# A linear and a sliding-window attention stack with its gradients on one core: another schedule for the window attention's backward, and phi's derivative made from stored features

## The chip, the core and the metric

The kernel runs on 1 of the 8 cores of one Trainium2 chip, in one launch. The metric is the device time of one execution in microseconds (us), of which several are taken; the median counts. A core has five engines that run their own instruction queues in order and wait for each other by semaphores: TensorE (matmuls, PE in the profile), VectorE (DVE), ScalarE (ACT), GpSimd (POOL) and SyncE (SP, which here only issues DMAs). ScalarE's queue issues some of the DMAs too. TensorE writes into PSUM, which has eight banks of 2 KB in each partition; VectorE and ScalarE read it from there.

## The reference

Four residual layers on x of shape [2048, 640], in the order A, B, A, B, with the weights of A used twice and those of B twice; then the gradients of x and of the four weight matrices by reverse differentiation, from a given `grad_out`. 32 heads of 20 columns each.

```python
def _A_ref(x, wqkv, wo):                       # linear attention
    q, k, v = ...                              # [32 heads, 2048, 20] each, of x @ wqkv
    phi = lambda t: jnp.where(t > 0, t + 1, jnp.exp(t)) + 1e-6
    pq, pk = phi(q), phi(k)
    kv = jnp.einsum("bhsd,bhse->bhde", pk, v)
    z = jnp.einsum("bhsd->bhd", pk)
    num = jnp.einsum("bhqd,bhde->bhqe", pq, kv)
    den = jnp.einsum("bhqd,bhd->bhq", pq, z)[..., None] + 1e-6
    return (num / den) ... @ wo

def _B_ref(x, wqkv, wo):                       # softmax attention, causal window of 256
    scores = jnp.einsum("bhqd,bhkd->bhqk", q, k) * (Dh ** -0.5)
    mask = (idx[:, None] - idx[None, :] >= 0) & (idx[:, None] - idx[None, :] < W)
    p = _softmax(jnp.where(mask[None, None], scores, -1e9), axis=-1)
    return jnp.einsum("bhqk,bhkd->bhqd", p, v) ... @ wo

x = x + _A_ref(_layernorm(x), A_wqkv, A_wo)    # and B, A, B in the same way
```

The derivative of phi is 1 where t > 0 and exp(t) elsewhere, that is min(exp(t), 1).

## The kernel before, in words

The 2048 rows are 16 tiles of 128 rows (index `tt`). Everything is bf16 with sums in float32. Layers count 0 (A), 1 (B), 2 (A), 3 (B).

**Forward (`forward`).** All work is recorded as operations with an engine, a guessed duration and what they read and write; `Sched` then plans them against each other and writes out the order of every engine (`emit`). Guessed times and the order in which operations were recorded decide, so taking some out can move others. For an A layer `a_qkv` makes the projections of a tile in chunks of 320 columns: ScalarE takes exp (L462), VectorE caps it at 1 (L463), which gives `e` = phi's derivative, and adds max(t, 1e-6) (L466), which gives the features. Features of q (`pq`), features of k beside v (`kv`), and `e` itself (320 KB a tile, L475) are stored to DRAM from SP's queue for the backward.

**Backward.** It alternates between a `bwd_phase` and the attention's backward `B_attn_bwd`: phase for layer 3, attention of layer 3, phase (layer 3's tail, layer 2, the start of layer 1), attention of layer 1, phase (layer 1's tail and layer 0). `bwd_phase` is planned by `Sched` as well. In it `lin_grads` makes dq, dk and dv of an A layer for each tile: six chunks of banded matmuls (L856), of which VectorE multiplies those of q and k by `e` (L1190) and ScalarE copies those of v (L1186). Before them `start` brings `dNT`, `kvT` and `ee` (the stored `e`, 320 KB) in by SP's queue. `tail` follows: `dh` by TensorE and ScalarE (L849, L997), then `scr` and `sm` on VectorE (L1005 to L1011), `w` on ScalarE (L1012), `gw` on GpSimd (L1015) and the carried gradient `gcar` on VectorE (L1017). In layer 2 `local_dO` comes behind it for the attention of layer 1: `slab` and `dd` on VectorE (L1058 to L1072), `prod` on GpSimd (L1065), and a store of `dOp` from ScalarE's queue (L1075).

**The attention's backward (`B_attn_bwd`).** Its order is written out by hand. Heads go in 8 groups of four. Within a group the steps are 15 blocks `n`, each of three 128x128 pieces of the band for four heads; a block has two pairs of heads, `h = 2n + p`. For each pair:

- `mm_s` makes scores into the tile `pair{h % 3}` (two banks, three such tiles), `act_exp` takes exp on ScalarE (L1351), GpSimd masks two of the three pieces (L1355, L1358).
- `mm_dp` writes dP over the scores, and `dve_ds` on VectorE (L1366) makes `ds` = exp x dP x scale in bf16.
- `ds` has to be transposed for dq: by `pe_turn` on TensorE (six transposes, L1384) into `dsT_ps` (two buffers of one bank), copied to SBUF by `copy_t` on VectorE or ScalarE (L1387), or by `dma_turn`, a DMA transpose on SP's queue. `by_dma` says for which blocks the second pair goes by DMA.
- The products (L1399, L1403) are narrow sums of 32 columns for dq, dk and dv. `pair_acc` lays them in the spare columns 384 to 480 of the tile `pair` that two pairs later holds scores and dP, and `pair_evac` takes them out to `dqkv` (128x120, L1387), on ScalarE or VectorE.

Each of these is given a place in time by a number of pairs in `ORDER`; they are sorted by it, and that is the order in every engine's queue. The loop that issues them:

Of the kernel before, what the change touches and what calls it, by code (L numbers as in the profile page):

```python
# [32 lines left out]
def dve_ns(n):  # L33
# [4 lines left out]
    ((0.3, 1.05, "ACT", 0.6, 1.6, "DVE"), (1.3, 2.25, "DVE", 0.6, 1.6, "ACT"), (2.3, 3.5, "DVE", 0.6, 1.05, "ACT")),  # L38
    ((0.7, 2.25, "DVE", 0.6, 1.3, "ACT"), (0.3, 1.8, "ACT", 0.6, 1.3, "ACT"), (2.05, 1.8, "DVE", 0.25, 1.3, "ACT")),
# [140 lines left out]
class Kern:  # L180
    def __init__(self, ctx, tc, x0, A_wqkv, A_wo, B_wqkv, B_wo, grad_out, outs):
# [69 lines left out]
        for l in (0, 2):  # L251
            self.sv[l] = dict(
                pq=d.tile([T, D], BF, name=f"pq{l}"), e=d.tile([T, 2 * D], BF, name=f"e{l}"),
# [57 lines left out]
    def forward(self):  # L311
# [7 lines left out]
        with ExitStack() as st:  # L319
# [120 lines left out]
            def a_qkv(l, tt, hnT):  # L440
# [3 lines left out]
                def chunk(ci):  # L444
                    def f():
# [362 lines left out]
    def bwd_phase(self, lb, la, nb, ahead=()):  # L808
# [8 lines left out]
        with ExitStack() as st:  # L817
# [82 lines left out]
            if wide:  # L900
                for name, n, shape, dt in (
                        ("dh", 1, [P, D], F32), ("w", 1, [P, D], F32), ("gw", 1, [P, D], F32), ("sm", 3, [P, 8], F32),
                        ("scr", 1, [P, D], BF), ("pq", 2, [P, D], BF), ("dNT", 2, [P, DT + 1, P], BF),
                        ("kvT", 2, [P, 2 * DT, P], BF), ("ee", 2, [P, 2 * D], BF)):
# [248 lines left out]
            def lin_grads(tt, items, t0):  # L1153
# [3 lines left out]

                def start():
# [4 lines left out]
                    c["ee"] = load("ee", sv["e"], tt)  # L1163

                def chunk(kind, ci):
                    def f():
# [18 lines left out]
                        if kind == "v":  # L1185
                            op("ACT", act_ns(CW), lambda: nc.scalar.copy(dst(), ps.t[:, 0:CW]), [ps],  # L1186
                               [("dqkv", tt, "v")])
                        else:
                            e, x0 = c["ee"], (D if kind == "k" else 0) + e0
                            op("DVE", dve_ns(CW), lambda: nc.vector.tensor_mul(dst(), ps.t[:, 0:CW], e.t[:, x0:x0 + CW]),  # L1190
                               [ps, e], [("dqkv", tt, kind)])
# [99 lines left out]
    def B_attn_bwd(self, l, dqkv, slab0=None, first=None):  # L1291
        nc, tc, D, T, TT, H, G, DP = self.nc, self.tc, self.D, self.T, self.TT, self.H, self.G, self.DP
        ld, E, DS, PR, TPS, TSB, ACC = {}, {}, {}, {}, {}, {}, {}
        with ExitStack() as st:
# [75 lines left out]
            def by_dma(n):  # L1370
                return n % NB not in (0, 2, 4, 6) and n < NS - 6
# [34 lines left out]
            def spare(h):  # L1406

                return PR[h][:, :, 3 * P:3 * P + 3 * HPAD].rearrange("p i (s c) -> p i s c", c=HPAD)

            def pair_acc(g, t, p, h):  # L1410
                if h not in PR:
                    PR[h] = pps.tile([P, 2, 512], F32, name=f"pair{h % 3}")
# [143 lines left out]
```

## Time and profile before

| | |
|---|---|
| median of 3 runs | 2328.52 us (2324.72 to 2328.61) |
| the profiled execution | 2327.18 us, of which the span from first to last instruction is 2325.2 us |
| mean granted TensorE clock | 0.945 |
| busy: PE, weight load | 2023.2 us (87%), 1405.2 us (60%) |
| busy: DVE, ACT, POOL | 1463.7 us (63%), 1182.6 us (51%), 852.3 us (37%) |
| DMA | 389.22 MB, 167 GB/s on the mean |
| attention backward, layers 3 and 1 | from 849.5 and from 1619 us, some 320 us each |
| `lin_grads` of layers 2 and 0 | from about 1381 and 2150 us |

Rows of groups read: line of the kernel, engine, operation, out<-in with shapes, count | busy us, mean ns of one | idle time of the engine just before them, and what ended it. A row of a timeline is start in us, duration in us, engine, line, operation, and in brackets how long the engine had been idle and for whom. A row of stretches gives, after start, end and length, busy us and count of PE, weight load, DVE, ACT and POOL, then granted clock, the busy share of the DMA engines and GB/s; asked for one line alone, it has that engine alone. Rows of waits give the waiting engine, tile and line, what it waited for, us in total, times and the longest. In a row of one line's instructions stand minimum, median and maximum in ns. A busy PE is not PE at its peak, since the ends of pipelined matmuls are modelled.

### The profile page before, as it was taken

What the parts mean: (1) busy time and instruction counts of PE and PEld (TensorE: products, weight loads), DVE (VectorE), ACT (ScalarE), POOL (GpSimd) and SP (SyncE); (2) the same over time, 40 slices, a digit from 0 to 9 for tenths busy, and PEclk for the clock granted to TensorE, in tenths of its full rate; (3) what the DMA queues carried; (4) which work ended last, traced back from release to release, by engine and by line L of the source; (5) the groups of instructions that cost most, each with busy time, mean ns of one, the idle gap of its engine ahead of it and who ended that gap; (6) DMA issues with size and microseconds to landing.
All of it is one profiled execution on the core that took longest, in us unless ns stands there. A gap on an engine that the chain in (4) does not pass through costs nothing. (4 is left out here: it accounts for less than half of the span.)

```text
span 2325.2 us, 67576 instructions
## 1 busy us (share of the span) xinstructions
PE 2023.2 (87%) x27798; PEld 1405.2 (60%) x27798; DVE 1463.7 (63%) x3048; ACT 1182.6 (51%) x2091; POOL 852.3 (37%) x1851
## 2 busy tenths in 40 slices
PE   6879899888887688888889979997888888998999
PEld 4556566555555456666656657754666665665674
DVE  6657677555564488898943328912998885443551
ACT  4527787527787137787832213311888783210330
POOL 1015455315666245555522203311555552221120
PEclk9989999879999798899999989998999899998999
DMA  7658999646675768898887789737898988987973
GB/s 256 198 140 192 209 203 216 169 125 161 151 157 126 197 165 150 136 155 147 155 192 171 160 191 196 181 85 157 147 151 148 148 147 171 193 187 177 214 171 100
DMA packets 968103, 389.22 MB, mean 167 GB/s; under 512 B 860401, under 2 KB 939889, under 8 KB 967537
## 3 DMA queue, kind: packets, MB, share of 16 engines
q1 hardware_dynamic: 931488, 351.24, 72.7%
q10 hardware_dynamic: 36304, 33.67, 4.5%
q8 instruction: 217, 3.56, 0.7%
q14 instruction: 94, 0.76, 0.1%
HBM read 115.34 MB, written 114.95 MB: 99 GB/s over the span
## 5 line engine op out<-in xcount | busy, mean ns | idle before, releaser
L1366 DVE SCALAR_TENSOR_TENSOR ds_sb<-pair,e_sb 128x768 bf16<-128x768 f32 x480 | 457.5, 954 | 79.9 <-ACT dqkv L1387 43.9
L1351 ACT ACTIVATE e_sb<-pair 128x768 bf16<-128x768 f32 x480 | 389.6, 813 | 144.8 <-PE pair L1331 134.3
L626 ACT ACTIVATE e_sb<-s_ps 128x1536 bf16<-128x1536 f32 (+2 forms) x256 | 350.8, 1370 | 91.9 <-PE s_ps L621 44.6
L630 POOL TENSOR_SCALAR_AFFINE_SELECT e_sb<-e_sb 128x256 bf16<-128x256 bf16 x512 | 216.9, 447 | 457.2 <-ACT e_sb L626 455.0
L849 PEld LDWEIGHTS <-om 128*128 128x128 bf16 x1920 | 191.3, 100 | 179.9 <-DMA om<-o 21.5
L849 PE MATMUL mm_ps<-wq,dqT 128*128 128x320 bf16 x1920 | 282.3, 302 | 10.4 <-DMA dqT<-dqkv 10.2
L1358 POOL TENSOR_SCALAR_AFFINE_SELECT e_sb<-e_sb 128x256 bf16<-128x256 bf16 x448 | 183.0, 408 | 259.0 <-ACT e_sb L1351 253.7
L849 PE MATMUL mm_ps<-dqkv,om 128*128 128x480 bf16 x1280 | 271.2, 370 | 0.0
L1015 POOL TENSOR_TENSOR gw<-w,gcar 128x640 f32<-128x640 f32 x64 | 89.6, 1399 | 457.2 <-ACT w L1012 442.9
L1331 PE MATMUL pair<-KTg,QTg 32*128 32x384 bf16 (+2 forms) x1024 | 169.6, 336 | 93.3 <-DVE ds_sb L1366 80.0
L1355 POOL TENSOR_SCALAR_AFFINE_SELECT e_sb<-e_sb 128x256 bf16<-128x256 bf16 x512 | 207.4, 408 | 86.1 <-ACT e_sb L1351 86.1
L849 PEld LDWEIGHTS <-dqT 128*128 128x128 bf16 x1920 | 186.1, 99 | 84.9 <-DMA dqT<-dqkv 11.0
L1399 PE MATMUL pair<-Ksl,dsT 128*128 128x32 bf16 x2712 | 217.7, 179 | 0.0
L1403 PE MATMUL pair<-Qsl,ds_sb 128*128 128x32 bf16 x2824 | 214.0, 177 | 0.0
L1403 PE MATMUL pair<-dOsl,e_sb 128*128 128x32 bf16 x2824 | 213.8, 177 | 0.0
L997 ACT ACTIVATE dh<-mm_ps 128x320 f32<-128x320 f32 x128 | 56.0, 438 | 304.4 <-PE mm_ps L849 238.1
L399 PE MATMUL mm_ps<-Wqkv_B,hnTB 128*128 128x320 bf16 x960 | 184.2, 308 | 5.4 <-DMA hnTB<-hnB 3.8
L655 PEld LDWEIGHTS <-e_sb 128*128 128x128 bf16 x2880 | 130.7, 97 | 81.2 <-DVE e_sb L635 18.5
L1399 PEld LDWEIGHTS <-dsT 128*128 128x128 bf16 x2880 | 153.2, 98 | 42.6 <-issue 42.6
L1331 PE MATMUL pair<-VTg,dOTg 32*128 32x384 bf16 (+2 forms) x1024 | 169.7, 337 | 10.0 <-DMA dOTg<-dOpt 7.0
L655 PE MATMUL pv_ps<-v_slab,e_sb 128*128 128x32 bf16 x2880 | 155.3, 178 | 22.0 <-POOL e_sb L638 6.6
L1384 PE MATMUL dsT_ps<-ident,ds_sb 128*128 128x128 bf16 x1896 | 171.3, 231 | 0.5 <-ACT dsT L1387 0.3
(154 smaller groups left out, 3705.3 us busy)
## 6 DMA issues: line engine op xcount, KB each, us to landing
qkvp<-qk_slab SPq DMA_DIRECT2D x32, 512.0 KB, 3.1
e<-ee SPq DMA_DIRECT2D x32, 320.0 KB, 2.5
kv<-kv SPq DMA_DIRECT2D x32, 320.0 KB, 2.7
o<-o SPq DMA_DIRECT2D x64, 160.0 KB, 3.2
om<-o SPq DMA_DIRECT2D x20, 512.0 KB, 4.7
hn<-hn SPq DMA_DIRECT2D x64, 160.0 KB, 2.9
om<-hn SPq DMA_DIRECT2D x20, 512.0 KB, 4.7
ee<-e SPq DMA_DIRECT2D x32, 320.0 KB, 3.6
```

What stands on the lines that cost most here:

```text
L399: nc.tensor.matmul(ps.t[:, w0:w0 + width], lhsT=lhsT(), rhs=rhs(), start=start, stop=stop)
L626: op("ACT", av(4 * nkt * P), lambda: nc.scalar.activation(e.t[:, :, 0:nkt, :], s.t[:, :, 0:nkt * P].rearrange("p h (i q) -> p h i q", q=P) ...
L630: op("POOL", 440, lambda p_=p_: nc.gpsimd.affine_select(out=e.t[:, 2 * p_:2 * p_ + 2, nkt - 1, :], in_=e.t[:, 2 * p_:2 * p_ + 2, nkt - 1, ...
L655: nc.tensor.matmul(pv.t[:, h % 16, :], lhsT=e.t[:, hh, j, :], rhs=vts[j].t[:, h, :], start=(j == 0), stop=(j == nkt - 1))
L849: nc.tensor.matmul(ps.t[:, w0:w0 + width], lhsT=lhsT(), rhs=rhs(), start=start, stop=stop)
L1331: nc.tensor.matmul(ps[:, i, c0:c0 + len(ks) * P], lhsT=ld[g][lhs][r, q * P:(q + 1) * P], rhs=ld[g][rhs][r, ks[0] * P:(ks[-1] + 1) * P], st ...
L1351: nc.scalar.activation(e, PR[h][:, :, 0:3 * P].rearrange("p i (j q) -> p i j q", q=P), ACT.Exp, scale=self.c_att)
L1355: nc.gpsimd.affine_select(out=e[:, :, j, :], in_=e[:, :, j, :], compare_op=ALU.is_ge, fill=0.0, base=0, pattern=[[0, 2], [-1, P]], channel ...
L1358: nc.gpsimd.affine_select(out=e[:, :, j, :], in_=e[:, :, j, :], compare_op=ALU.is_ge, fill=0.0, base=-1, pattern=[[0, 2], [1, P]], channel ...
L1366: nc.vector.scalar_tensor_tensor(out=DS[n][:, hs], in0=PR[h][:, :, 0:3 * P].rearrange("p i (j q) -> p i j q", q=P), scalar=self.c_att, in1 ...
L1399: nc.tensor.matmul(out(hh, 0), lhsT=TSB[2 * n + hh // 2][:, hh % 2, j, :], rhs=ld[g]["K"][:, k, cs], start=(i == 0), stop=(i == len(dq) - 1))
L1403: nc.tensor.matmul(out(hh, 1 + x), lhsT=src[n][:, hh, j, :], rhs=ld[g][rhs][:, q, cs], start=(i == 0), stop=(i == len(dkv) - 1))
```

## The change

Two things at once. In the attention's backward the narrow sums get a bank of their own, `dqvk_ps`, for all four heads of a tile, which ScalarE takes out once (128x240); to have that bank, `dsT_ps` has one buffer where it had two. `by_dma` is true for the odd blocks of a group, 7 of 15 (it was 11). `ORDER` has new places, and `act_exp` comes at h + 0.4 (it was 0.7). And `e` is neither stored nor loaded: for each tile of `lin_grads`, `phi` loads the features of q and of k (160 KB each) by ScalarE's queue into a tile of `ee`, which has three buffers (it had two), and `slope` makes min(feature - 1e-6, 1) of them on VectorE, two instructions of 128x640.

```diff
 ORDER = (
-    ((0.3, 1.05, "ACT", 0.6, 1.6, "DVE"), (1.3, 2.25, "DVE", 0.6, 1.6, "ACT"), (2.3, 3.5, "DVE", 0.6, 1.05, "ACT")),
-    ((0.7, 2.25, "DVE", 0.6, 1.3, "ACT"), (0.3, 1.8, "ACT", 0.6, 1.3, "ACT"), (2.05, 1.8, "DVE", 0.25, 1.3, "ACT")),
+    ((0.05, 1.8, "DVE", 1.05), (1.05, 1.06, "ACT", 1.05)),
+    ((0.05, 1.8, "DVE", 1.05), (None, None, None, 0.6)),
 )
...
-                        if ci == 3:
-                            dma("SP", lambda: self.tm_view(sv["e"])[:, tt, :], lambda: e.t, 320 * KB,
-                                [(e, i) for i in range(4)], [])
...
+                def phi():
+                    c["ee"] = R["ee"].buf()
+                    for i, src in enumerate((sv["pq"], sv["kv"][:, 0:D])):
+                        dma("ACT", lambda i=i: c["ee"].t[:, i, :], lambda src=src: self.tm_view(src)[:, tt, :], 160 * KB,
+                            [], [(c["ee"], i)])
+
+                def slope():
+                    for i in (0, 1):
+                        op("DVE", 300, lambda i=i: nc.vector.tensor_scalar(
+                            out=c["ee"].t[:, i, :], in0=c["ee"].t[:, i, :], scalar1=1e-6, scalar2=1.0,
+                            op0=ALU.subtract, op1=ALU.min), [], [(c["ee"], i)])
...
-                    c["ee"] = load("ee", sv["e"], tt)
...
+                items.append((t0 - 1.1, phi))
                 items.append((t0 - 0.6, start))
+                items.append((t0 - 0.1, slope))
...
             def by_dma(n):
-                return n % NB not in (0, 2, 4, 6) and n < NS - 6
+                return n % NB % 2 == 1 and n < NS - 6
...
-                ps = TPS[h] = pps.tile([P, 2, 3, P], BF, name="dsT_ps", bufs=2)
+                ps = TPS[h] = pps.tile([P, 2, 3, P], BF, name="dsT_ps")
...
+            def acc(g, t, hhs):
+                if (g, t) not in ACC:
+                    ACC[g, t] = pps.tile([P, 3, 4, HPAD], F32, name="dqvk_ps")
+                products(g, t, hhs, lambda hh, x: ACC[g, t][:, x, hh, :])
+
+            def evac(g, t):
+                o = 4 * g * DH
+                copy("ACT", dqkv[:, t, :].rearrange("p (s x) -> p s x", s=3)[:, :, o:o + 4 * DH].rearrange(
+                    "p s (h d) -> p s h d", d=DH), ACC.pop((g, t))[:, :, :, 0:DH])
...
-                    kind = 0 if not by_dma(n) else 2 if by_dma(n + 1) else 1
-                    turn, cp, cp_eng, acc, ev, ev_eng = ORDER[p][kind]
+                    turn, cp, cp_eng, narrow = ORDER[p][by_dma(n)]
...
-                        at(h + 0.7, act_exp, h + 3)
+                        at(h + 0.4, act_exp, h + 3)
...
-                            at(h + max(turn, cp) + 0.01, copy_t, h, cp_eng)
+                            at(h + cp, copy_t, h, cp_eng)
                     units = outs.get(n, [])
-                    if len(units) == 2 and not p:
-                        at(h + acc + 0.01, quad_acc, *units[0])
-                        at(h + acc + 0.62, quad_evac, *units[0], "ACT")
-                    for g, t in units[-1:]:
-                        at(h + acc, pair_acc, g, t, p, h + 2)
-                        at(h + ev, pair_evac, g, t, p, h + 2, ev_eng)
+                    heads = (0, 1) if p == 0 else (2, 3)
+                    if len(units) == 2:
+                        units, heads = [units[p]], range(4)
+                    for o in units:
+                        at(h + narrow, acc, *o, heads)
+                        if heads[-1] == 3:
+                            at(h + 1.3, evac, *o)
```

More of the change, by code (lines that the diff above doesn't have):

```diff
@@ L252, in __init__ @@
             self.sv[l] = dict(
-                pq=d.tile([T, D], BF, name=f"pq{l}"), e=d.tile([T, 2 * D], BF, name=f"e{l}"),
+                pq=d.tile([T, D], BF, name=f"pq{l}"),
                 kv=d.tile([T, 2 * D], BF, name=f"kv{l}"), o=d.tile([T, D], BF, name=f"o{l}"),
@@ L1188, in f @@
                         else:
[L1189 to L1191 removed]
+                            e, i = c["ee"], int(kind == "k")
+                            op("DVE", dve_ns(CW), lambda: nc.vector.tensor_mul(dst(), ps.t[:, 0:CW], e.t[:, i, e0:e0 + CW]),
+                               [ps, (e, i)], [("dqkv", tt, kind)])
                     return f
+                items.append((t0 - 1.1, phi))
                 items.append((t0 - 0.6, start))
+                items.append((t0 - 0.1, slope))
                 for i, (kind, ci) in enumerate((k, ci) for k in "qkv" for ci in range(2)):
```

19 lines of the change are left out of this document (1 added, 18 removed).

## The prediction

> **What bounds the kernel now.** I read the stretches by engine first, then the groups, then the timelines of the two places that the change touches.
>
> Busy time by stretch (columns PE, PE weight load, VectorE, ScalarE, GpSimd, granted clock, DMA share, GB/s); the first two rows are the attention backward of layers 3 and 1, the third is the pass over `lin_grads` of layer 2, the fourth that of layer 0:
>
> ```profile
> 849.50:1172.40 322.90, 280.54 (x6177) 221.60 (x6177) 286.00 (x395) 255.46 (x481) 183.49 (x479) 0.92 0.86 150
> 1619.00:1937.00 318.00, 273.61 (x6164) 218.02 (x6164) 284.65 (x394) 254.48 (x479) 182.05 (x474) 0.96 0.90 150
> 1381.50:1512.00 130.50, 124.33 (x1140) 93.43 (x1138) 107.41 (x235) 40.79 (x110) 38.60 (x28) 0.99 0.88 190
> 2150.00:2260.00 110.00, 104.11 (x952) 78.10 (x951) 63.73 (x156) 40.65 (x109) 20.99 (x15) 0.97 0.93 198
> ```
>
> In the attention stages VectorE is 89% and 90% busy, with GpSimd and ScalarE in one loop with it. VectorE's `ds` there shows the beat: 15 blocks (30 pairs) take 39.3 us at full clock, 2.62 us a block, and more where the clock is down:
>
> ```profile
> 849.50:891.80 42.30, 28.52 (x31) 0.71 0.84 148
> 1015.50:1054.80 39.30, 28.55 (x30) 1.00 0.93 151
> ```
>
> What the 15 blocks of the second row hold, by group, and two rows of the waits:
>
> ```profile
> L1366 DVE SCALAR_TENSOR_TENSOR ds_sb<-pair,e_sb 128x768 bf16<-128x768 f32 x30 | 28.6, 954 | 3.9 <-ACT dqkv L1387 2.4 <-issue 0.8 <-POOL e_sb L1358 0.4
> L1351 ACT ACTIVATE e_sb<-pair 128x768 bf16<-128x768 f32 x30 | 24.4, 813 | 6.6 <-PE pair L1331 6.2
> L1384 PE MATMUL dsT_ps<-ident,ds_sb 128*128 128x128 bf16 x114 | 9.6, 220 | 0.0
> L1387 DVE COPY dsT<-dsT_ps 128x768 bf16<-128x768 bf16 x16 | 8.8, 548 | 0.0
> L1387 ACT CAST dqkv<-pair 128x120 bf16<-128x120 f32 x26 | 6.7, 258 | 0.8
> L1387 ACT COPY dsT<-dsT_ps 128x768 bf16<-128x768 bf16 x4 | 3.2, 792 | 0.0
> ...
> PE pair L1331 <- DVE ds_sb L1366: 38.9, 103, 0.8
> ...
> DVE ds_sb L1366 <- ACT dqkv L1387: 23.5, 68, 0.8
> ```
>
> 114 transposes are 19 pairs turned by TensorE (six each); the other 11 go by DMA. The last two rows are of the whole first stage (us in total, times, longest us), and the last is the one the change removes: 68 times `ds` stands until the narrow sums in its own `pair` tile have been taken out. In this timeline (start, us) one such wait, and the slots: an engine's next instruction starts a little before the recorded end of the one in front.
>
> ```profile
> 1036.22 0.96 DVE L1366 SCALAR_TENSOR_TENSOR ds_sb<-pair,e_sb 128x768 bf16<-128x768 f32 x1 [0.16 <-ACT dqkv L1387]
> 1037.10 0.55 DVE L1387 COPY dsT<-dsT_ps 128x768 bf16<-128x768 bf16 x1
> ...
> 1036.49 0.81 ACT L1351 ACTIVATE e_sb<-pair 128x768 bf16<-128x768 f32 x1 [0.37 <-PE pair L1331]
> 1037.65 0.81 ACT L1351 ACTIVATE e_sb<-pair 128x768 bf16<-128x768 f32 x1
> 1038.36 0.25 ACT L1387 CAST dqkv<-pair 128x120 bf16<-128x120 f32 x1
> ...
> 1036.12 0.34 PE L1331 MATMUL pair<-KTg,QTg 32*128 32x384 bf16 x2 [0.44 <-DVE ds_sb L1366]
> 1036.39 0.51 PE L1384 MATMUL dsT_ps<-ident,ds_sb 128*128 128x128 bf16 x6
> 1036.74 0.23 PE L1399 MATMUL pair<-Ksl,dsT 128*128 128x32 bf16 x3
> ...
> 1038.53 0.41 POOL L1358 TENSOR_SCALAR_AFFINE_SELECT e_sb<-e_sb 128x256 bf16<-128x256 bf16 x1 [0.39 <-ACT e_sb L1351]
> 1038.89 0.41 POOL L1355 TENSOR_SCALAR_AFFINE_SELECT e_sb<-e_sb 128x256 bf16<-128x256 bf16 x1
> ...
> 1018.84 0.55 DVE L1387 COPY dsT<-dsT_ps 128x768 bf16<-128x768 bf16 x1
> 1019.31 0.95 DVE L1366 SCALAR_TENSOR_TENSOR ds_sb<-pair,e_sb 128x768 bf16<-128x768 f32 x1
> 1016.20 0.79 ACT L1387 COPY dsT<-dsT_ps 128x768 bf16<-128x768 bf16 x1
> 1016.91 0.81 ACT L1351 ACTIVATE e_sb<-pair 128x768 bf16<-128x768 f32 x1
> 1022.07 0.38 ACT L1387 CAST dqkv<-dsT_ps 128x240 bf16<-128x240 f32 x1
> 1022.33 0.83 ACT L1351 ACTIVATE e_sb<-pair 128x768 bf16<-128x768 f32 x1
> ```
>
> Slots: `ds` 0.87, VectorE copy 0.47, exp 0.71, ScalarE copy 0.71, a 128x240 take-out 0.27. TensorE: scores with dP 0.27, a turn 0.35, a pair's narrow sums about 0.45 to 0.5. Scores start to exp: 0.37. Exp end (1037.65 + 0.81 = 1038.46) to both masks done (1039.30): 0.84.
>
> **The attention part, step by step.** Narrow sums move to a bank of their own, taken out once a block by ScalarE; `dsT_ps` falls to one buffer; 7 of 15 second pairs go by DMA instead of 11.
>
> VectorE over two blocks (one odd, one even): 4 `ds` x 0.87 + 2 copies x 0.47 = 4.42; its take-outs (4 per 15 blocks) are gone. ScalarE: 4 x 0.71 + 2 x 0.27 + 1 copy x 0.71 = 4.09. TensorE: 4 x 0.27 + 3 turns x 0.35 + 4 x 0.45 = 3.9. GpSimd: 8 masks x 0.36 = 2.9. All lie under 2 x 2.62 = 5.24, so the loop between them decides, and I lay it out from the first `ds` of an odd block at 0, with 0.05 for a semaphore and 0.2 until PSUM can be read. For the third pair: scores at 0.25, once the turn in front is through; exp 0.64 to 1.45; masks done 2.32: third `ds`. For the fourth: the first `ds` frees its tile at 0.96, scores 1.01, exp only at 1.63 behind the take-out, 2.44, masks 3.31: fourth `ds`. For the fifth: ScalarE copies the odd pair's turn at 2.34, exp at 3.04 to 3.85, masks 4.72. VectorE: `ds` 0, copy 0.87, `ds` 1.33, 2.32, 3.31, copy 4.19, `ds` 4.72. Its own work would have allowed 4.42; the loss of 0.3 is behind the masks. So 2.36 us a block; 7.5 x 4.72 = 35.4, and with the two even blocks that meet at a group's end 35.9. Laid out the same way, the old order gives 39.5 beside the measured 39.3, so the steps are about right. With 0.53 for the narrow sums it is 36.6 after and 40.2 before: the difference holds at 3.5 us a group, 8.9%.
>
> The one buffer of `dsT_ps`: a turn waits for the copy of the turn in front, and scores, dP and sums queue behind it on TensorE. It has 0.38 us a block to spare, so I cost it at nothing beyond the layout. Fewer DMA turns (11 to 7 a group) take load off a DMA share of 0.86 to 0.90; the slab loads stay, and no `ds` waited for them, so nothing either.
>
> At half clock TensorE is the longest, and there four more turns a group cost 4 x 0.69 = 2.8 us. The clock column gives (1 - 0.92)/0.5 x 322.9 = 52 us and (1 - 0.96)/0.5 x 318 = 25 us at half rate. So 8.9% of 641 - 77 = 564 us, 50 us, is gained, and 77/58 of a group (58 us is 15 blocks of the layout at half clock) x 2.8 = 4 us lost. I take 46 to 48: **-47 us**, bounds -68 (full clock all along, worked out below) and 0 (the loop stays as it is).
>
> The clock rows are half against a rule of the Trainium skill, "TensorE: Matmul & The Clock Gate", section "Part 1: The HAM clock gate": the half rate is the idle state and sustained activity of some 3.4 us lifts it. TensorE's longest stand behind `ds` in this stage was 0.8 us, and the first 42 us of it still have a clock of 0.71, so the trace doesn't bear the rule out alone. By it a fuller TensorE would run at full clock, and the sum would be that of the second rival below.
>
> **phi's derivative, layer 2.** Here the beat is a serial chain:
>
> ```profile
> 1438.78 1.95 DVE L1017 SCALAR_TENSOR_TENSOR gcar<-hn,sm,gw 128x640 bf16<-128x640 bf16 x1 [0.36 <-POOL gw L1015]
> 1439.57 0.44 ACT L997 ACTIVATE dh<-mm_ps 128x320 f32<-128x320 f32 x1 [1.67 <-PE mm_ps L849]
> 1442.16 0.30 DVE L1072 SCALAR_TENSOR_TENSOR slab<-dd,slab 128x32 bf16<-128x32 f32 x1
> 1442.49 0.35 ACTq L839 DMA_DIRECT2D dOpt<-slab  x1
> 1442.89 0.44 ACT L997 ACTIVATE dh<-mm_ps 128x320 f32<-128x320 f32 x1 [2.79 <-DVE dqkv L1190]
> 1443.45 0.82 DVE L1005 CUSTOM_DVE_ANT_0 scr<-dh,hn 128x640 bf16<-128x640 f32 x1 [0.28 <-ACT dh L997]
> 1446.97 1.95 DVE L1017 SCALAR_TENSOR_TENSOR gcar<-hn,sm,gw 128x640 bf16<-128x640 bf16 x1 [0.36 <-POOL gw L1015]
> L463 DVE TENSOR_SCALAR ee<-ee x64: 190/234/245, 13.5 to 118.3; 128x320 bf16<-128x320 bf16 x64
> L434 DVE TENSOR_SCALAR hnA<-x,mv,rs 128x640 bf16<-128x640 bf16 x32 | 14.7, 459 | 0.8 <-ACT rs L433 0.6
> ```
>
> From one `gcar` to the next 8.19 us: `gcar`, `dd`, `slab`, the store of `dOp` in ScalarE's queue, `dh` behind it, `scr`, `w`, GpSimd's `gw`, `gcar`. In the changed kernel's order of instructions both new subtractions stand right behind `gcar`, inside this chain. Price of one: between 0.23 (128x320) and 0.46 (128x640 with two pointer scalars); it is nearest the first with twice the columns, about 0.32, a slot of 0.24. So 2 x 0.24 x 13 steps that have this chain = **+6 us**, bounds 0 and 2 x 0.46 x 16 = +15. ScalarE's 32 new loads stand ahead of the first `dh`, the row at 1439.57, where it idles 1.67 us for TensorE; two issues of 0.35 (the store's row) fit there, and the buffer that they wait for was freed a tile before. The 32 loads of `e` on SP (320 KB) go and the same bytes come in 64 halves. In layer 0 VectorE is busy 63.7 of 110 us and TensorE 104: the 32 subtractions (16 x 2 x 0.24 = 8 us) and loads are covered; were TensorE to wait for them they would cost that 8.
>
> **The forward.** 32 stores of 320 KB leave SP's queue; the planner puts some matmuls in another order. The longest row of waits for a DMA in the stage where half of them lie (175 to 440 us) is small:
>
> ```profile
> PEld L399 <- DMA oTA<-oA: 9.0, 6, 3.0
> ```
>
> I take -1 us, bounds -8 (most of these 9 us) and +6 (a worse order, as much as the one above).
>
> **Sum.** -47 + 6 - 1 = -42 on the profiled execution's 2327.18 us: 2285. The median of the runs is 2328.52, 0.06% above it; 0.2% (4.7 us) is about what this kernel's measurement can tell from no change.
>
> **Rivals.**
> Smaller gain: the loop is longer than laid out, through later masks or TensorE waiting for the single banks, by 0.1 us a block: 240 x 0.1 = 24 us less, 2309. For it: all three waits of the layout hang on GpSimd's masks. Against: the same steps meet 39.3 for the old order.
> Full clock: nothing at half rate, 16 x 3.5 plus the 12 us that the half clock now adds (641 - 16 x 39.3) = -68, with +6 and -1: 2264. For it a TensorE with more to do: 15 x 2 x (0.27 + 0.45) + 23 x 0.35 = 29.7 of 35.9 us, 83%, where 19 turns in 39.3 make 72%. Against it the 0.71 above.
> Slower: the one bank of narrow sums. The next block's sums wait for the take-out, which stands behind an exp. Loop: sums 0.45, turn, scores and dP 0.63, sums 0.45, 0.2, semaphores 0.1, take-out 0.38 = 2.2 us a block plus the wait for ScalarE. It decides from 2.62 - 2.2 = 0.42 us on; with a whole exp in front (0.81) a block takes 3.0, at 0.6 it takes 2.8 and the stages 240 x 0.18 = 43 us more: 2375. My layout has waits of 0.05 to 0.33.
> No effect: the loop is held by something that stays, 2327 + 6 - 1 = 2332 or, with the forward, 2327.
>
> **Chances.** Forecast 0.56 (2272 to 2300), full clock 0.12, smaller gain 0.14, no effect 0.05 (of which 0.03 within 0.2%), slower 0.13. Faster 0.82, same 0.03, slower 0.15. The range takes the first three: 2262 to 2320.
>
> **What would show it.** `ds` should come every 1.18 us on the mean with 15 blocks in about 36 us; its wait for a take-out should be gone, with short waits for GpSimd's masks in their place; 2244 transposes of `ds` on TensorE instead of 1896; 256 take-outs of 0.38 on ScalarE. In layer 2 `gcar` to `gcar` about 8.65. A wait of TensorE's sums for ScalarE's take-out, or of the turn for a copy, of over 0.4 us in every block would make it wrong.

## The result, and the profile after

The changed kernel takes 2320.25 us (median of 14 runs, 2316.67 to 2327.12), the kernel before beside it 2327.41 us (14 runs): a ratio of 0.9971, 95% interval 0.9957 to 0.9985. Some 7 us were gained where 42 were forecast. The profiled execution of the changed kernel took 2323.05 us with a span of 2321.1 us, 4.1 us less than the span before.

Between the two profiled executions 4 us were gained of 42 forecast. To see where the other 38 went, I divided both spans at the same events: the first and last `ds` of each attention stage, the last `dNx` behind it (the end of `tail` and `lin_dO`), the first and last product of `lin_grads`, each by its start. In us:

| stretch | before | after | difference | forecast |
|---|---|---|---|---|
| start to first `ds` (forward, local phase) | 849.5 | 847.3 | -2.2 | -1 |
| first to last `ds`, layer 3 | 321.9 | 301.3 | -20.6 | -47 for both |
| last `ds` to last `dNx` | 182.5 | 189.6 | +7.1 | 0 |
| last `dNx` to first product, layer 2 | 27.6 | 27.4 | -0.2 | 0 |
| first product to next stage's `ds`, layer 2 | 237.5 | 245.4 | +7.9 | +6 |
| first to last `ds`, layer 1 | 317.2 | 301.9 | -15.3 | with layer 3 |
| last `ds` to last `dNx` | 185.4 | 192.4 | +7.0 | 0 |
| last `dNx` to last product, layer 0 | 127.6 | 139.3 | +11.7 | 0 |
| last product to end | 76.0 | 76.5 | +0.5 | 0 |

The stretches by engine of the changed kernel, for the same four places as in the prediction (columns as there):

```profile
847.30:1148.60 301.30, 293.88 (x6320) 216.00 (x6319) 283.29 (x371) 252.91 (x414) 182.66 (x478) 0.98 0.77 139
1611.00:1912.90 301.90, 293.48 (x6316) 216.12 (x6317) 283.30 (x372) 252.51 (x413) 181.22 (x474) 0.97 0.74 136
1373.00:1511.00 138.00, 126.99 (x1129) 94.13 (x1130) 114.27 (x257) 40.20 (x108) 39.95 (x29) 0.98 0.78 171
2134.00:2255.00 121.00, 104.91 (x956) 78.25 (x955) 82.15 (x183) 40.61 (x109) 20.96 (x15) 0.96 0.90 178
```

The attention stages are 20 and 15 us shorter, TensorE is recorded as busy for 97% of them, and the granted clock rose from 0.92 and 0.96 to 0.98 and 0.97. In layer 0 TensorE has the same 104 us of work as before, spread over some 11 us more.

`ds` alone (start and end, length, busy us and count, clock, DMA share, GB/s), and rows of the waits of the first stage:

```profile
875.00:1125.00 250.00, 191.00 (x201) 1.00 0.76 137
1660.00:1885.00 225.00, 171.86 (x181) 1.00 0.77 137
```

```profile
POOL e_sb L1368 <- ACT e_sb L1361: 111.1, 222, 1.8
ACT e_sb L1361 <- PE pair L1341: 43.2, 80, 1.8
...
DVE ds_sb L1376 <- POOL e_sb L1365: 12.3, 39, 3.0
...
DVE ds_sb L1376 <- PE dsT_ps L1394: 5.0, 15, 0.3
```

201 `ds` in 250 us are one per 1.244 us, 37.3 us for 15 blocks (39.3 before, 35.9 forecast). The 23.5 us for which `ds` stood behind the take-outs are gone; in their place stand 12.3 us for GpSimd's masks (4.0 before) and 5 us put down to the turns, which the layout of the prediction had as well, but smaller. VectorE's order over two blocks:

```profile
1016.56 0.96 DVE L1376 SCALAR_TENSOR_TENSOR ds_sb<-pair,e_sb 128x768 bf16<-128x768 f32 x1
1017.44 0.55 DVE L1397 COPY dsT<-dsT_ps 128x768 bf16<-128x768 bf16 x1
1017.90 0.95 DVE L1376 SCALAR_TENSOR_TENSOR ds_sb<-pair,e_sb 128x768 bf16<-128x768 f32 x1
1019.05 1.92 DVE L1376 SCALAR_TENSOR_TENSOR ds_sb<-pair,e_sb 128x768 bf16<-128x768 f32 x2 [0.20 <-POOL e_sb L1365]
1020.89 0.55 DVE L1397 COPY dsT<-dsT_ps 128x768 bf16<-128x768 bf16 x1
1021.49 0.96 DVE L1376 SCALAR_TENSOR_TENSOR ds_sb<-pair,e_sb 128x768 bf16<-128x768 f32 x1
```

Two blocks take 1021.49 - 1016.56 = 4.93 us. The slots of four `ds` and two copies are 4.42, so VectorE loses 0.51: 0.28 in front of the third `ds` (1.15 from start to start where 0.87 is its slot), 0.10 between third and fourth (1.84 for the two), 0.13 behind the second copy. The layout had the same order and 0.30.

Five rows around the first of these `ds`, of the copy ahead of it and of the other engines, show where the third `ds` loses its time:

```profile
1015.97 0.55 DVE L1397 COPY dsT<-dsT_ps 128x768 bf16<-128x768 bf16 x1
...
1016.57 0.50 PE L1394 MATMUL dsT_ps<-ident,ds_sb 128*128 128x128 bf16 x6
1017.00 0.34 PE L1341 MATMUL pair<-KTg,QTg 32*128 32x384 bf16 x2
...
1017.38 0.81 ACT L1361 ACTIVATE e_sb<-pair 128x768 bf16<-128x768 f32 x1 [0.56 <-PE pair L1341]
...
1018.61 0.41 POOL L1365 TENSOR_SCALAR_AFFINE_SELECT e_sb<-e_sb 128x256 bf16<-128x256 bf16 x1
```

The turn starts 0.05 us behind the end of the copy that empties the only `dsT_ps` (1015.97 + 0.55 = 1016.52). The scores stand behind the turn in TensorE's queue, exp comes after the scores, the masks (until 1019.02) after exp, and the third `ds` at 1019.05 after the masks. Between 875 and 1125 us, 60 of the 107 turns that follow a VectorE copy start within 0.1 us of its end; in the kernel before, with two buffers, none of 98 does.

The places that were forecast at nothing. ScalarE and VectorE at the start of the phase behind layer 3's attention:

```profile
1154.99 0.36 ACT L1397 CAST dqkv<-dqvk_ps 128x240 bf16<-128x240 f32 x1 [0.76 <-PE dqvk_ps L1413]
...
1156.82 1.32 ACTq L836 DMA_DIRECT2D ee<-pq  x1
...
1160.76 0.44 ACTq L836 DMA_DIRECT2D ee<-kv  x1
1161.25 0.44 ACT L994 ACTIVATE dh<-mm_ps 128x320 f32<-128x320 f32 x1 [5.91 <-DMA ee<-kv]
...
1160.87 1.20 DVE L1163 TENSOR_SCALAR ee<-ee 128x640 bf16<-128x640 bf16 x3 [2.42 <-DMA ee<-pq]
...
1163.69 0.33 DVE L1163 TENSOR_SCALAR ee<-ee 128x640 bf16<-128x640 bf16 x1 [0.58 <-DMA ee<-pq]
1163.93 0.82 DVE L1002 CUSTOM_DVE_ANT_0 scr<-dh,hn 128x640 bf16<-128x640 f32 x1
```

Six loads of features (1156.82 to 1161.2) stand in ScalarE's queue ahead of the phase's first `dh`, and five subtractions that wait for them stand on VectorE ahead of the first `scr`. From the last `ds` to the first `dh` it is 12.6 us (6.6 before), to the first `gcar` 18.8 us (12.5). In layer 0 the rows of waits and of DMAs point at one thing. TensorE's waits for the transposed `dqkv` that the next `dh` reads (us in total, times, longest), before and after:

```profile
PE mm_ps L849 <- DMA dqT<-dqkv: 5.9, 3, 5.1
```

```profile
PE mm_ps L846 <- DMA dqT<-dqkv: 15.1, 6, 8.5
```

and the median time of these transposes from issue to landing, before and after:

```profile
dqT<-dqkv SPq DMA_TRANSPOSE x16, 3.4
```

```profile
dqT<-dqkv SPq DMA_TRANSPOSE x16, 4.8
```

They land 1.4 us later, and TensorE stands 9 us longer for them.

### The profile page after: what moved, and what is told of

Its sections match the earlier page's. It is cut to its first block, busy times and chain, and to the rows that moved or that the text cites. A ratio compares the mean times of both kernels' runs of the same rounds, so it can differ in the third digit from the quotient of the medians.

```text
span 2321.1 us, 68252 instructions
## 1 busy us (share of the span) xinstructions
PE 2059.7 (89%) x28146; PEld 1400.7 (60%) x28146; DVE 1488.6 (64%) x3060; ACT 1178.4 (51%) x1959; POOL 849.2 (37%) x1851
## 5 line engine op out<-in xcount | busy, mean ns | idle before, releaser
L846 PEld LDWEIGHTS <-om 128*128 128x128 bf16 x1920 | 192.0, 101 | 179.9 <-DMA om<-o 20.2
L846 PEld LDWEIGHTS <-dqT 128*128 128x128 bf16 x1920 | 185.9, 99 | 99.3 <-DMA dqT<-dqkv 25.6
L1409 PE MATMUL dqvk_ps<-Ksl,dsT 128*128 128x32 bf16 x2880 | 225.7, 178 | 2.7 <-ACT dqkv L1397 2.7
L1413 PE MATMUL dqvk_ps<-dOsl,e_sb 128*128 128x32 bf16 x2880 | 220.3, 177 | 0.2 <-issue 0.2
L1413 PE MATMUL dqvk_ps<-Qsl,ds_sb 128*128 128x32 bf16 x2880 | 220.2, 177 | 0.0
L1394 PE MATMUL dsT_ps<-ident,ds_sb 128*128 128x128 bf16 x2244 | 191.8, 223 | 7.0 <-DVE dsT L1397 1.9
L399 PE MATMUL mm_ps<-Wqkv_B,hnTB 128*128 128x320 bf16 x960 | 185.9, 310 | 8.3 <-DMA hnTB<-hnB 6.8
L1409 PEld LDWEIGHTS <-dsT 128*128 128x128 bf16 x2880 | 146.1, 96 | 66.9 <-issue 66.9
L1341 PE MATMUL pair<-VTg,dOTg 32*128 32x384 bf16 (+2 forms) x1024 | 164.6, 325 | 18.5 <-DMA dOTg<-dOpt 6.7
L1341 PE MATMUL pair<-KTg,QTg 32*128 32x384 bf16 (+2 forms) x1024 | 163.1, 328 | 6.8 <-DMA KTg<-qkvp 5.5
```

Of the source, the lines that this page charges most:

```text
L399: nc.tensor.matmul(ps.t[:, w0:w0 + width], lhsT=lhsT(), rhs=rhs(), start=start, stop=stop)
L846: nc.tensor.matmul(ps.t[:, w0:w0 + width], lhsT=lhsT(), rhs=rhs(), start=start, stop=stop)
L1341: nc.tensor.matmul(ps[:, i, c0:c0 + len(ks) * P], lhsT=ld[g][lhs][r, q * P:(q + 1) * P], rhs=ld[g][rhs][r, ks[0] * P:(ks[-1] + 1) * P], st ...
L1394: nc.tensor.transpose(ps[:, i, j, :], DS[n][:, 2 * p + i, j, :], self.ident)
L1409: nc.tensor.matmul(out(hh, 0), lhsT=TSB[2 * n + hh // 2][:, hh % 2, j, :], rhs=ld[g]["K"][:, k, cs], start=(i == 0), stop=(i == len(dq) - 1))
L1413: nc.tensor.matmul(out(hh, 1 + x), lhsT=src[n][:, hh, j, :], rhs=ld[g][rhs][:, q, cs], start=(i == 0), stop=(i == len(dkv) - 1))
```

## The experiments

The theory after reading both traces: the attention part is worth 36 us, and phi's derivative gives most of that back, by its loads in ScalarE's queue more than by its subtractions. The rival is that the subtractions do it, or that the two parts spoil each other. Where a kernel is timed, the ratio is to the kernel before on the same chip; the medians of the kernel before were 2324.64, 2330.74 and 2330.79 us in the three sets.

**The attention part alone** (`ORDER`, `dqvk_ps`, `by_dma`, as in the diff above; `e` stored and loaded as before).

> The attention part of the change alone; e is stored and loaded as before. Theory: the two attention stages give what they gave in the changed kernel, 21 + 15 = 36 us, and each loses some 2 us between its last ds and the first dh behind it, where the single bank of narrow sums is filled and emptied in turn (6.2 us there against 4.2): 32 us faster than before, ratio 0.986, and from a last ds to the first gcar 14 to 15 us (12.5 before, 18.8 changed). Rival: the whole of the 7 us that the changed kernel loses behind each attention stage belongs to this part: 22 us faster, ratio 0.991, and 18 to 19 us from ds to gcar.

Measured: 2298.66 us, ratio 0.9889 (0.9861 to 0.9916). The stages take 301.7 and 301.5 us, 20.2 and 15.7 less. From the last `ds` to the first `dh` 8.4 us, to the first `gcar` 14.5 us, as the theory has it; from `ds` to the last `dNx` 4.2 and 1.2 us more than before. The interval holds the rival's ratio, and the theory's 0.986 lies at its edge; the 14.5 us decide for the theory: about a third of the changed kernel's delay of `gcar` (2.0 of 6.3 us) is of this part.

**Phi's derivative alone** (the other half of the diff).

> phi's derivative made from loaded features alone, on the attention of before. Theory: 5 us lost behind each attention stage (six loads in ScalarE's queue and six subtractions on VectorE ahead of the first dh and scr), 8 us in layer 2, 12 us in layer 0, 2 us won in the forward: 26 to 28 us slower, ratio 1.0115. Rival, as the prediction had it: 5 us slower (6 in layer 2, the rest covered), ratio 1.002, the other losses being of the attention part or of both together.

Measured: 2361.35 us, ratio 1.0156 (1.0129 to 1.0182), 36 us slower: 8.8 in layer 2, 15.7 in layer 0, 5.4 and 1.5 behind the attention stages, 3.2 in the forward. The prediction's 5 us for this part is refuted, and the 26 to 28 us expected here were too few as well. The differences of the two spans from the kernel before add up to +7.3 us, against the -4.1 of both together. Of these 11.4 us, 7.2 lie in the forward; this kernel's is the same program as the changed kernel's and took 852.7 us where that took 847.3, so much of it is scatter. The rest is open.

**No subtractions.** q's and k's features go into the products as they are.

```diff
-                items.append((t0 - 0.1, slope))
```

> The changed kernel without the two subtractions (q's and k's features are multiplied in where phi's derivative belongs), loads as they are. If the loads in ScalarE's queue cost layer 0 its 12 us, they stay; layer 2 loses its 8 us and the phase starts about 2.5 each: 13 us faster than the changed kernel, 2307, ratio to before 0.991. If the subtractions on VectorE are what layer 0 and the phase starts pay for: 8 + 12 + 10 = 30 us faster than the changed kernel, 2290, ratio 0.984.

Measured: 2310.57 us, ratio 0.9941 (0.9921 to 0.9961). Layer 0's products take 113.3 us (110.2 changed, 99.3 before): the whole loss stays without a single subtraction. Layer 2's stretch is 240.5 us, 4.9 less than with them; the first `gcar` comes after 17.1 and 16.1 us, 1.6 to 1.7 earlier. So the subtractions cost about what the prediction gave them in layer 2, and nothing in layer 0. The time lies above both forecasts (2307 was the theory's): layer 2 and the phase starts gave less than expected.

**The loads in SP's queue.**

```diff
-                        dma("ACT", lambda i=i: c["ee"].t[:, i, :], lambda src=src: self.tm_view(src)[:, tt, :], 160 * KB,
+                        dma("SP", lambda i=i: c["ee"].t[:, i, :], lambda src=src: self.tm_view(src)[:, tt, :], 160 * KB,
```

> The changed kernel with the loads of features in SP's queue instead of ScalarE's (160 KB each as before; the order on VectorE moves with it at the phase starts). If the loads' place in ScalarE's queue and their own DMA ring beside the transposes of dqT are the cause: layer 0 falls back by 8 to 12 us, each phase start by 5, layer 2 keeps its 8: 2300, ratio 0.988. If the subtractions are the cause: layer 0 keeps its 12 us and only the phase starts gain: 2310, ratio 0.9925.

Measured: 2299.73 us, ratio 0.9897 (0.9862 to 0.9933). Layer 0's products are back at 100.0 us with all subtractions in place, layer 2 keeps most of its loss (243.9). The first `gcar` comes after 16.2 and 14.5 us (18.8 and 17.7 changed). One word in the kernel is worth some 17 us by the two ratios; the interval holds the rival's ratio too, and layer 0's products decide. In layer 0 TensorE waits 7.4 us in all for `dqT` (15.1 changed), and the transposes land sooner:

```profile
dqT<-dqkv SPq DMA_TRANSPOSE x15, 3.8
```

SP's order and ScalarE's tell why. First SP's queue of this kernel, then SP's and ScalarE's of the kernel without subtractions (start, us to issue):

```profile
2164.29 1.26 SPq L840 DMA_TRANSPOSE dqT<-dqkv  x1
2165.60 0.92 SPq L836 DMA_DIRECT2D ee<-pq  x1
```

```profile
2165.37 1.25 SPq L840 DMA_TRANSPOSE dqT<-dqkv  x1
2165.29 0.33 ACTq L836 DMA_DIRECT2D ee<-pq  x1
2165.65 0.44 ACTq L836 DMA_DIRECT2D ee<-kv  x1
```

The products that `dqT` waits for are the ones that set a buffer of `ee` free. In one queue the load is issued behind the transpose; from ScalarE's it starts at the same moment. The Trainium skill, "DMA: Bandwidth & Descriptors", section "Queues, rings and completion order", says that SP and ScalarE have a ring each on the same 16 DMA engines, and that an engine takes packets from the rings in turn. The trace agrees as far as it goes: with the loads beside them the transposes land 1.0 to 1.4 us later on the median (4.8 us against 3.8 and 3.4).

**The load of `e` in ScalarE's queue**, on the attention part alone: nothing of phi's derivative but the queue.

```diff
-                    c["ee"] = load("ee", sv["e"], tt)
+                    c["ee"] = R["ee"].buf()
+                    dma("ACT", lambda: c["ee"].t, lambda: self.tm_view(sv["e"])[:, tt, :], 320 * KB, [], [c["ee"]])
```

> The attention part alone, e stored as before, but the load of e (320 KB) in ScalarE's queue instead of SP's. No subtraction, no halves, two buffers as before. If a load in ScalarE's queue is what holds up the transposes of dqT in layer 0: its products take 110 to 118 us (100.2 with the load in SP's queue, 99.3 before), the transposes of dqT 4.9 us or more to landing (3.8), layer 2 some 3 us more: 2312, ratio 0.9935. If it was the halves, the third buffer or the subtractions: 100 us and 2298, ratio 0.988.

Measured: 2310.94 us, ratio 0.9915 (0.9891 to 0.9939). Layer 0's products take 111.3 us (100.2 with the load in SP's queue), and layer 2's stretch 240.4 (237.7). The transposes land after 4.5 us (4.9 or more expected), and TensorE waits for them as in the changed kernel:

```profile
PE mm_ps L849 <- DMA dqT<-dqkv: 16.6, 4, 9.9
```

So a load in ScalarE's queue is enough; halves, third buffer and subtractions aren't needed for layer 0's loss, and in layer 2 the queue is worth 2.7 us.

**The loads later in ScalarE's queue.**

```diff
+                    behind = [("g", TT - 1)] if tt < 3 else [("g", tt - 5)] if tt > 4 else []
...
-                            [], [(c["ee"], i)])
+                            behind, [(c["ee"], i)])
```

> The changed kernel with the same loads of features in ScalarE's queue and the same subtractions, but the loads planned behind a gcar: in layers 2 and 0 they stand behind the store of gcar or dOp instead of right behind the copies of v, and the first three tiles' come at the end of the tails in front instead of at the start of the phase. If the loads hurt by their moment (released by the same products as the transposes of dqT, and ahead of the first dh): layer 0's products take 100 to 103 us again (110.2 changed, 99.3 before), the first gcar comes 14 to 15 us after the last ds (18.8 and 17.7 changed): 2302, ratio 0.989. If they hurt because they run in a DMA ring of their own beside the transposes, whenever they come: layer 0 stays at 110 to 115, and only the phase starts gain: 2312, ratio 0.9935.

Measured: 2326.03 us, ratio 0.9976 (0.9964 to 0.9988). Both theories fell on the time. The first `gcar` does come after 14.5 us in both phases, and the transposes of `dqT` land after 3.7 us, which points to the moment as what held them up. But layer 0's products take 117.9 us, for another reason:

```profile
2195.05 1.56 ACTq L836 DMA_DIRECT2D ee<-pq  x1
2196.65 0.67 ACTq L836 DMA_DIRECT2D ee<-kv  x1
2197.37 0.44 ACT L994 ACTIVATE dh<-mm_ps 128x320 f32<-128x320 f32 x1 [4.07 <-PE mm_ps L853]
...
2197.93 0.82 DVE L1002 CUSTOM_DVE_ANT_0 scr<-dh,hn 128x640 bf16<-128x640 f32 x1 [2.11 <-ACT dh L994]
```

The loads now stand behind the store of `gcar` and ahead of the `dh` that the chain is waiting for; two issues took 2.2 us here, and `scr` and TensorE stood for it. In this kernel's row of waits from 2124 to 2245 us that adds up:

```profile
DVE scr L1002 <- ACT dh L994: 12.3, 11, 2.1
```

What was won at the phase starts was mostly lost again before the last `dNx` (6.1 and 4.7 us more than before).

**The last three tiles' sums in the `pair` tiles**, on the attention part alone.

```diff
-                    ACC[g, t] = pps.tile([P, 3, 4, HPAD], F32, name="dqvk_ps")
+                    if g == G - 1 and t + 2 >= NB:
+                        ACC[g, t] = pps.tile([P, 2, 512], F32, name=f"pair{t % 3}")[:, 0, 0:12 * HPAD].rearrange(
+                            "p (s h c) -> p s h c", s=3, c=HPAD)
+                    else:
+                        ACC[g, t] = pps.tile([P, 3, 4, HPAD], F32, name="dqvk_ps")
```

> The attention part of the change alone (e stored as before), with the narrow sums of the last three tiles of the last group in the three pair tiles, which are free by then, instead of one bank in turn. If the filling and emptying of the single bank is what the attention part pays behind each stage: from the last ds to the first dh 6.6 us again (8.4 with the attention part alone), 2 us less in each phase, 2294, ratio to before 0.987. If the later dh comes of something else: 8.4 stays, 2298, ratio 0.989.

Measured: 2296.9 us, ratio 0.9853 (0.9833 to 0.9873). From the last `ds` to the first `dh` 7.2 us (8.4), to the last `dNx` 184.6 and 185.9 us, 2.1 and 0.7 less than with the single bank. This row of the attention part alone, three waits of 0.45 us behind the last `ds`, is not among this kernel's waits:

```profile
PE dqvk_ps L1399 <- ACT dqkv L1387: 1.3, 3, 0.5
```

So the single bank costs some 1.2 us of delay at each stage's end, and the rival of the prediction by which it would slow the whole loop is not seen.

**One of two masks**, on the changed kernel: the far edge of the window isn't masked in the backward.

```diff
-                    elif k == t - 2:
-                        nc.gpsimd.affine_select(out=e[:, :, j, :], in_=e[:, :, j, :], compare_op=ALU.is_ge, fill=0.0,
-                                                base=-1, pattern=[[0, 2], [1, P]], channel_multiplier=-1)
```

> The changed kernel with one of GpSimd's two masks left out (the far edge of the window isn't masked, in the backward alone). If the masks' end is what VectorE waits for in the attention loop: 15 blocks take 34 to 35.5 us (37.3 changed; VectorE's own 30 ds and 16 copies make 33.6) and each stage is 28 to 50 us shorter: 2235, ratio 0.962 (0.95 to 0.97). If TensorE bounds the loop by now (recorded busy for 98% of it): 15 blocks stay within 0.4 of 37.3 and the time at 2314 to 2320, ratio 0.996.

Measured: 2313.15 us, ratio 0.9925 (0.9902 to 0.9949). `ds` of the same window:

```profile
875.00:1125.00 250.00, 193.38 (x205) 1.00 0.77 139
```

36.6 us for 15 blocks, 0.7 less, although half of GpSimd's work is gone (a slot of 0.36 us a pair, some 10 us in 15 blocks). The rival gave at most 0.4, so neither fits. The rows of waits of the first stage tell why:

```profile
DVE ds_sb L1373 <- PE pair L1341: 11.3, 47, 0.7
DVE ds_sb L1373 <- POOL e_sb L1365: 6.0, 16, 3.0
```

`ds` waits less for the masks (12.3 us in the changed kernel), and 11.3 us for TensorE's scores and dP, for which the changed kernel has 0.5. The masks do come last in the changed kernel, but a second path lies close behind them.

**A third of the sums of dk and dv**, on the changed kernel: only the last of three matmuls is made.

```diff
-                        for i, (q, n, j) in enumerate(dkv):
+                        for i, (q, n, j) in enumerate(dkv[-1:]):
                             nc.tensor.matmul(out(hh, 1 + x), lhsT=src[n][:, hh, j, :],
-                                             rhs=ld[g][rhs][:, q, cs], start=(i == 0), stop=(i == len(dkv) - 1))
+                                             rhs=ld[g][rhs][:, q, cs], start=True, stop=True)
```

> The changed kernel with a third of the narrow sums of dk and dv (one matmul of three each: 16 matmuls fewer of 36 a block, about 0.4 us of TensorE a block; dk and dv of layers 3 and 1 are incomplete). If TensorE's queue sets the attention loop: 15 blocks take 34 to 35 us (37.3 changed, 36.7 without a mask; VectorE's own work makes 33.6) and each stage is 20 to 28 us shorter: 2275, ratio 0.978. If the loop is a chain through VectorE, ScalarE and GpSimd that TensorE's amount of work doesn't lengthen: 36.9 to 37.3, 2316 to 2320, ratio 0.9965.

Measured: 2320.88 us, ratio 0.9963 (0.9948 to 0.9977). `ds`, and TensorE, of this kernel:

```profile
875.00:1125.00 250.00, 191.87 (x202) 1.00 0.73 138
870.00:1140.00 270.00, 235.30 (x4152) 1.00 0.74 140
```

37.1 us for 15 blocks, with 4152 matmuls where the changed kernel has 5814 in the same 270 us. The amount of TensorE's work doesn't bound the loop, although TensorE was recorded as busy for 98% of it. `ds` waits for the masks as in the changed kernel:

```profile
DVE ds_sb L1376 <- POOL e_sb L1365: 11.6, 39, 3.0
```

Each of the two experiments left the other path as it was. A kernel with fewer masks and fewer sums at once wasn't tried.

**Products with min in one instruction, loads in SP's queue.**

```diff
-                items.append((t0 - 0.1, slope))
...
-                            op("DVE", dve_ns(CW), lambda: nc.vector.tensor_mul(dst(), ps.t[:, 0:CW], e.t[:, i, e0:e0 + CW]),
+                            op("DVE", dve_ns(CW), lambda: nc.vector.scalar_tensor_tensor(
+                                out=dst(), in0=e.t[:, i, e0:e0 + CW], scalar=1.0, in1=ps.t[:, 0:CW], op0=ALU.min,
+                                op1=ALU.mult),
```

> The changed kernel with the features loaded by SP's queue and no subtractions: the products of q and k take min(feature, 1) x sum in one instruction (the 1e-6 is left in). If the subtractions in the chain of gcar are layer 2's loss: from the first product of layer 2 to the next stage 237 to 239 us (237.5 before, 245.4 changed, 243.9 with SP's queue alone), layer 0 100 us, 2294, ratio 0.987. If the combined instruction is slower than the plain product (0.49 us) by 0.1 us or more, four a tile in the chain, layer 2 stays at 243 to 246: 2300, ratio 0.990.

Measured: 2295.47 us, ratio 0.9849 (0.9827 to 0.9871). Layer 2's stretch is 238.5 us (243.9 with subtractions and SP's queue), layer 0's products 100.9. The combined instruction is no longer than the product (484 ns in the changed kernel):

```profile
L1192 DVE SCALAR_TENSOR_TENSOR dqkv<-ee,mm_ps 128x320 bf16<-128x320 bf16 x54 | 24.8, 481 | 15.9 <-PE mm_ps L853 15.7
```

**This with the `pair` tiles at the end.**

> The changed kernel with features loaded by SP's queue, min and product in one instruction, and the last three tiles' narrow sums in the pair tiles. If the gains of these add up (2 us of the drain in the first phase, 1 in the second, over the 2295 of the kernel with the one instruction): 2292, ratio 0.9835. If the drain was hidden by something else in this kernel: 2295, ratio 0.985.

Measured: 2292.93 us, ratio 0.9836 (0.9815 to 0.9857). The first `gcar` comes after 13.3 and 13.2 us (14.4 without), but layer 0's products took 104.9 us, 4 more, for a cause that stays open. The intervals can't tell this kernel from the one without the `pair` tiles; against both kernels of the case it is 1.6% and 1.3% faster.

**And with 11 second pairs turned by DMA.**

```diff
-                return n % NB % 2 == 1 and n < NS - 6
+                return n % NB not in (0, 2, 4, 6) and n < NS - 6
```

> As the one before, but with 11 of 15 second pairs turned by DMA as in the kernel before (7 in the changed one): four turns fewer on TensorE and eight copies fewer on VectorE in 15 blocks, four copies more on ScalarE, and more DMA. If TensorE's and VectorE's amount of work sets the loop: 15 blocks in 35.5 to 36.5 us, 2280, ratio 0.978. If ScalarE does where two DMA blocks follow each other (two exps, a take-out and a copy, 2.4 us of slots a block, and its waits), or the later DMA turns: 37.3 to 39, 2292 to 2318, ratio 0.983 to 0.994.

Measured: 2291.24 us, ratio 0.9831 (0.9807 to 0.9855), the same as the one before within the intervals, and at the edge of the second forecast. `ds`:

```profile
875.00:1125.00 250.00, 194.25 (x204) 1.00 1.06 162
```

36.8 us for 15 blocks: four turns and eight VectorE copies (8 x 0.47 = 3.8 us) fewer bring 0.5 us, at a DMA share of 1.06; the loop lies between the two forecasts. The stages are 4 and 5 us shorter, but in this execution the forward, the same program, took 9.9 us longer. Layer 0's products took 104.7 us again.

## Why the prediction was wrong

By its own steps, in the order of the sum:

- **Attention, -47: right in kind, -36 measured.** Order, copies, turns (2244) and take-outs came as laid out, the wait for the take-out went, and short waits for masks came. The loop is 37.3 us for 15 blocks, not 35.9, 0.2 us more per two blocks. The step that failed is "scores at 0.25, once the turn in front is through", and with it the one buffer of `dsT_ps`, costed at nothing. Counted from the `ds` at 1016.56, the turn starts at 0.01, the scores at 0.44, exp at 0.82 (0.64 laid out), and the masks are done at 2.46 (2.32). The layout's own numbers give the delay: its copy at 4.19 lasts 0.55 and so ends 0.02 behind the `ds` at 4.72; with 0.05 for the semaphore and 0.35 for the turn the scores can't start before 0.42. This is read from the trace; no run has a second buffer, and with the three `pair` tiles, `dsT_ps` and `dqvk_ps` all eight banks are taken.

  The beat gives 16 x (39.3 - 37.3) = 32 us. The remaining 4 go with the higher clock, though no run shows that it is the cause: the stages lay 10.3 us above 16 x 39.3 before and 6.4 above 16 x 37.3 after. So the rival "smaller gain" (0.1 us a block) happened in the loop, for the single bank of the turns and the later masks that it names, and perhaps a part of the rival "full clock" beside it. Taking work from one engine brings little: half of GpSimd's masks 0.7 us in 15 blocks, 16 of 36 sums on TensorE 0.2, eight VectorE copies and four turns together with more ScalarE copies 0.5. ScalarE's work was never taken away. By the trace the beat is a closed round of copy, turn, scores, exp, masks, `ds` and the next copy (1015.97 to 1020.89, the 4.9 us of two blocks), but no experiment shortened that round alone.
- **Layer 2, +6: right for the subtractions.** `gcar` to `gcar` is 8.65 us, the number forecast:

```profile
1437.25 1.95 DVE L1014 SCALAR_TENSOR_TENSOR gcar<-hn,sm,gw 128x640 bf16<-128x640 bf16 x1 [0.35 <-POOL gw L1012]
...
1445.90 0.88 DVE L1014 SCALAR_TENSOR_TENSOR gcar<-hn,sm,gw 128x640 bf16<-128x640 bf16 x1 [0.35 <-POOL gw L1012]
```

  The stretch lost 7.9 us; taking the subtractions out gave 4.9 (ScalarE's queue) and 5.4 (SP's) of it. Most of the rest are the loads in ScalarE's queue, which the prediction had at nothing because ScalarE idles for TensorE there: taking them out of it gave 1.5 us (with subtractions) and 2.0 (without).
- **Layer 0, 0: the largest loss in one stretch (11.7 us).** That the 32 subtractions and loads "are covered" is true of the subtractions. The loads were judged by room in ScalarE's queue and by bytes, which stay the same; that leaving SP's queue lets them run beside the transposes of `dqT`, which TensorE waits for, wasn't asked. The row for it was there: TensorE waited 5.9 us for `dqT` before.
- **The phase starts, 0: not looked at (14.1 us).** The loads have no dependency, so the planner put the first six at the very start of each phase, ahead of `dh`, with their subtractions ahead of `scr`. The prediction spoke only of the place in layer 2 where two issues fit. The other part is the bank of narrow sums, which was costed inside the loop but not at its end: with the attention part alone the first `gcar` came 2.0 us later, of which 1.2 go with the `pair` tiles. Up to the last `dNx` the attention part alone loses 5.4 us of the 14.1, phi's derivative alone 6.9.
- **Forward, -1: not to be told from one execution.** The four traces that store `e` reach the first `ds` at 849.5 to 853.5 us (mean 851.4), the ten that don't at 841.0 to 852.7 (mean 846.9): some -4, within the bounds given.

-35.9 + 14.1 + 7.7 + 11.7 - 2.2 + 0.5 = -4.1 us, the difference of the spans. The forecast of "faster" held, its size didn't: phi's derivative, which was to cost 5 us, costs 19 beside the attention part (ratio 0.9971 against 0.9889) and 36 alone, and with SP's queue next to nothing (0.9897). Why it costs less beside the attention part is, apart from the scatter, open.

## What to carry to other kernels

A load that is moved to another engine's DMA queue loses its place behind the transfers of the old queue: ask which transfer is issued at the same moment, and who waits for that one. A load without a dependency will be issued as early as its queue allows, so look at what stands behind it in that queue at the start of a phase, not only in the steady loop. An engine recorded as busy for 98% need not be held by its amount of work: take work from it, and look at the beat and at who is waited for then. A buffer given up belongs in the layout of a loop: its copy, the next writer and all that stands behind that writer in its queue.

## What the runs showed of the hardware

- **A subtraction of 0.32 us can take 1.47.** Of the 64, the shortest took 312 ns and the median 318, the longest 1471; in layer 0 their mean was 786 ns. There they run beside GpSimd's `gw`:

```profile
2191.49 1.40 POOL L1012 TENSOR_TENSOR gw<-w,gcar 128x640 f32<-128x640 f32 x1 [7.43 <-ACT w L1009]
2191.64 1.67 DVE L1163 TENSOR_SCALAR ee<-ee 128x640 bf16<-128x640 bf16 x2
2193.23 0.87 DVE L1014 SCALAR_TENSOR_TENSOR gcar<-hn,sm,gw 128x640 bf16<-128x640 bf16 x1
```

  `gw` ends at 2192.89, and the pair of subtractions 0.42 us later. It cost nothing here, since `gcar` waits for `gw` anyway and starts 0.34 us behind its end, where 0.35 is usual. The Trainium skill, "SBUF — State Buffer", section "SBUF: two separate sides", says that VectorE and GpSimd share a pair of ports, and that an instruction that needs the pair holds it to its end while the other engine's waits. The rows agree with that: the subtractions go on only until 0.42 us behind `gw`.
- **The clock.** From 870 to 1140 and 1650 to 1880 us the granted clock is 1.00 in all twelve kernels with the new order and 0.91 to 0.98 in the two with the old one. How full TensorE is over such a stretch doesn't tell the two apart well: with a third of the dk and dv sums it is busy for 235.3 of 270 us at 1.00, before for 232.3 at 0.92. The rule that the prediction weighed (the Trainium skill, "TensorE: Matmul & The Clock Gate", section "Part 1: The HAM clock gate") had the right sign here, more work and the full clock, but a share of busy time of 87% against 86% hardly explains 1.00 against 0.92. What does wasn't tried.
- **Which queue the loads stand in is worth 10 us in layer 0** at nearly the same bytes (20.7 to 21.0 MB in the products' stretch of the kernel before, the changed one and the one with SP's queue).
